# A convolution that feeds a mixture of experts: the third group's first stage moved ahead of the second sort, and what goes with it

## The chip, the cores and the metric

The kernel runs on one core of a Trainium2 chip. The metric is the device time of one execution in microseconds; the time of a kernel is the median of its runs. PE is the matrix engine (PEld its weight loads), DVE the vector engine, ACT the scalar engine, POOL the GpSimd engine. SP computes nothing here; it issues most of the DMA transfers, in the order of its queue. Every engine executes its own queue in order and waits there on semaphores.

## The reference, cut

Eight sequences of 5696 tokens of 128 channels are convolved causally with one filter per channel (by FFT in the reference). All 45568 tokens then go through a layer of eight experts, of which each token takes one.

```python
L = 2 * S
y = np.fft.irfft(np.fft.rfft(x, n=L, axis=1) * np.fft.rfft(h, n=L, axis=0)[None], n=L, axis=1)[:, :S]
t = y.reshape(B * S, D)
logits = t @ w_gate
expert_idx = np.argmax(logits, axis=1)          # gate_w = softmax probability of that expert
for e in range(E):
    mask = expert_idx == e
    out[mask] = gate_w[mask, None] * (np.maximum(t[mask] @ w1[e], 0.0) @ w2[e])
```

## The kernel before

The sequences are worked on in three groups of 2, 3 and 3. A sequence is laid out as a grid (48 by 119, padded to 120), so that the long Fourier transform becomes a transform over 120 points, one over 48 points and their inverses, all as matmuls. For each group there are these stages, which hand over through DRAM:

- `phase_a` (by `steps_a`): x to U, the first stage. An item is a quarter-slab of one sequence (`load` L287 brings `xt`, 240 KB; `cut` L278 splits it on ACT and DVE; `transform` L300 does three matmuls `pa` of 512 columns; `store` L309 copies `ut` by ACT and DVE). An item has two steps. When all sequences of a group have a slab, `flush` (L296) sends `ut` to U on SP, 720 KB at a time (L298).
- `phase_b`: U to V, the 48-point stage. Work goes by blocks `qb` of frequencies; `load_m` (L447) brings the matrices `mt`, by SP for the first two blocks of the third group and by POOL's queue behind them (`PLAIN` = 2); `load` (L468) brings `uq`, `mi` and the filter's spectrum `hh`, in two copies on the two halves of the partitions (L480). `forward` gives `xp` (two matmuls), `product` three DVE operations (L551, L560, L556), `combine` (L563) adds two of them, on DVE for the first `ALONE[g]` = (0, 14, 10) items and on POOL behind them, `inverse` gives `vp`, `save` (L591) has ACT copy it to `vt`.
- `phase_c`, the sort: V to tokens. `divide`, `synth` (matmul `yp`), `settle`, `turn`, `score` and `route` find each token's expert, `rank` (L872) finds its place and `sort` (L664) scatters the tokens there by POOL's indirect DMA. Behind every scatter but the last ones POOL sets a buffer to zero to pace the scatters (L896); this lies in `hh`'s third buffer, or in the first group in one of `mi`.
- `tables`: 12 short pieces of DVE work that make, from the counts per expert, the list of which tile of 256 tokens belongs to which expert.
- `experts`: a tile's tokens come as `xr`, an expert's weights as `wb` (SP, L1134). A step is one slice of 256 of the 1024 hidden units: `layer1` (`mh`), two relus (L1171 on ACT, L1173 on DVE), `layer2` (`ma`). A tile takes four steps, and there are 728 steps in all.

The first group's `phase_a` and `phase_b` come first. The first sort is then interleaved with the second group's `phase_a`. From there on `experts` runs beside `rest` (L1307), which does the second group's `phase_b`, the second sort, the third group's `phase_b` and the third sort. The third group's `phase_a` is a `Guest` (L351) of the second sort: it gets two steps (sometimes one) beside each piece of it, 72 in all. The interleaving is written out at build time: `run` (L1331) gives each stream a virtual time, and the next instructions are those of the stream that is behind. `HEAD` says when the experts start beside a group, `GAP` is a pause before the second and third sorts, in which only the experts get on, `SHARES` are the streams' shares.

In PSUM `vp` and `xp` share four banks (tag `cx`); the experts' `mh` has two banks of its own. `fcs` and `gcs` are constants of the two 120-point stages, read only at the beginning.

Of the kernel before, what the change touches and what calls it, by code (L numbers as in the profile page):

```python
# [23 lines left out]
NB = 48  # L24
# [3 lines left out]
HP = 64  # L28
# [23 lines left out]
ALONE = (0, 14, 10)  # L52
HEAD = (0, 5500, 9000)
# [13 lines left out]
TABLED = 4  # L67
RATE = (0.372, 0.55, 0.28, 0.8, 1.05, 0.6)
# [3 lines left out]
def conv_moe(ctx: ExitStack, tc: tile.TileContext, I, out, B, S, D, E, F, split):  # L72
# [86 lines left out]
    state = {"rests": False, "space": False, "spare": None, "pe": 0.0, "sent": 0.0, "tail": 0}  # L159

# [13 lines left out]
    fcs = load_const("fcs", [MP, 2, QN])  # L174
# [16 lines left out]
    gcs = load_const("gcs", [QN, 2, MP])  # L191
# [7 lines left out]
    jrow = load_const("jrow", [1, total])  # L199
# [66 lines left out]
    def steps_a(gr, tag, bufs):  # L266
        g, nb = gr.g, gr.nb
        srcs = [(I["x"][gr.b0 + b], b) for b in range(nb)]
        tw = 4 * D
        items = []  # L270
        for ig in range(NB // 4):
            for src, b in srcs:
                items.append((ig, src, b))
# [4 lines left out]
        def cut(n):  # L278
            if not split or n >= len(items):
                return  # L280
# [6 lines left out]
        def load(n):  # L287
            if n >= len(items):
                return
            ig, src, b = items[n]  # L290
# [18 lines left out]
        def store(m):  # L309
            n, c = divmod(m, 2)  # L310
            ig, src, b = items[n]
            if b == 0:
                uts[c] = sb.tile([QN, 4, gr.cols], F32, tag=tag, name=f"ut{g}_{ig}_{c}", bufs=bufs)
# [11 lines left out]
        def begin(m):  # L325
            if m == 0:
                cut(0)
            if m % 2 == 0:
                load(m // 2 + fore)
                cut(m // 2 + 1)  # L330
            transform(m)

        return start, begin, store, flush, 2 * len(items)

    def phase_a(gr):
        start, begin, store, flush, M = steps_a(gr, "six", SIX - gr.g)
        half = AT if gr.g == 0 else 750 * RATE[3 * gr.g - 3]
        start()
        for m in range(M + 2):
# [4 lines left out]
            yield half  # L344
# [6 lines left out]
    class Guest:  # L351
        def __init__(self, gr):
            self.start, self.step, self.store, self.flush, self.M = steps_a(gr, "mt", MT)
# [87 lines left out]
    def phase_b(gr):  # L441
# [26 lines left out]
        def load(qb):  # L468
# [8 lines left out]
            if g != 0:  # L477
                hhs[qb] = hhbufs[qb % 3]
                for k in range(2):
# [5 lines left out]
        state, banks, late = {}, {}, []  # L485

# [81 lines left out]
        def inverse(n):  # L568
# [4 lines left out]
            vp = ps.tile([P, 512], F32, tag="cx", name=f"vp{g}_{q}_{c}", bufs=4)  # L573
# [54 lines left out]
        for n in range(N + lags[3] + 2):  # L628
            qb, at = divmod(n, per)
            for k0 in range(at * PK, (at + 1) * PK):  # L630
                if k0 == 1:
                    load_m(qb + (3 if g == 0 else 2))
                if k0 == min(3, per * PK - 1):
                    load(qb + 2)
                if k0 == 0:
# [79 lines left out]
    def phase_c(pt, guest=None):  # L715
# [156 lines left out]
        def rank(n):  # L872
# [576 lines left out]
```

## Time and profile before

| | us |
|---|---|
| median of 3 runs | 2156.97 |
| lowest, highest run | 2149.70, 2160.83 |
| profiled execution, its own time | 2157.51 |
| its span in the trace | 2155.7 |
| PE busy in the span | 2082.7 |
| DVE busy | 1542.5 |
| ACT busy | 1114.9 |
| POOL busy | 1350.0 |

The span runs from the first to the last instruction of the trace. Stages in it: the first group until 229, the first sort and the second group's first stage from 229 to 391, the second group's 48-point stage from 394 to 685, a pause to 702, the second sort to 961, the third group's 48-point stage from 935 to about 1340, the third sort to about 1630, and experts alone behind it. A busy engine in the profile is one with an instruction in flight, and matmuls are pipelined: a row's count of instructions has to be read beside its busy time. In a row of instructions, the part in brackets is the idle time of the engine just before, and what ended it.

### The profile page before, as it was taken

The page shows a single profiled execution, that of the slowest core. Times are in us where ns is not written, and L with a number is a line of the kernel's source. Part 1 is how long each engine was busy: PE and PEld are TensorE (multiplying, and loading weights), DVE is VectorE, ACT ScalarE, POOL GpSimd, SP SyncE. Part 2 cuts the span into 40 slices and gives each one's busy share as a digit, 9 for nine tenths or more (in the row PEclk, how much of TensorE's full clock was granted, in tenths as well). Part 3 has the DMA queues.
Part 4 walks back from the last instruction along what each step waited for, and adds up shares of the span by engine and source line. Part 5 has one row for each costly group of instructions (what it writes and reads, how often), then busy time and mean ns, then how long its engine had stood idle before and what let it go on. Part 6 is the DMA issues. An engine that isn't in the chain of part 4 may idle for free.

```text
span 2155.7 us, 47101 instructions
## 1 busy us (share of the span) xinstructions
PE 2082.7 (97%) x14452; PEld 1863.3 (86%) x14452; DVE 1542.5 (72%) x3373; ACT 1114.9 (52%) x2317; POOL 1350.0 (63%) x1569
## 2 busy tenths in 40 slices
PE   9999999799999999989999999999999999999998
PEld 7799777377777889878888888999999999999998
DVE  4698677799997777688888887666665555555554
ACT  5677555143334666534555555555544454444544
POOL 6566388545554388888998775288883444443333
PEclk9999999599999999999999999999999999999999
DMA  8899799999997898868878885656533244343331
GB/s 269 263 289 293 227 297 281 256 237 256 248 267 196 232 276 255 245 168 229 204 205 222 216 203 153 159 132 159 141 103 98 87 132 135 129 133 126 123 121 34
DMA packets 216993, 420.33 MB, mean 195 GB/s; under 512 B 32501, under 2 KB 136235, under 8 KB 216740
## 3 DMA queue, kind: packets, MB, share of 16 engines
q1 hardware_dynamic: 187263, 360.52, 59.7%
q0 software_dynamic: 27072, 55.35, 8.9%
q8 instruction: 117, 1.92, 0.4%
q10 hardware_dynamic: 2405, 1.43, 0.2%
q14 instruction: 136, 1.11, 0.2%
HBM read 582.45 MB, written 154.27 MB: 342 GB/s over the span
## 4 chain that ended last, share of the span: by engine, by line
PE 82%; DMA 9%; DVE 3%; POOL 2%; issue 2%; ACT 1%; SPq 1%; ACTq 0%; POOLq 0%; DVEq 0%
PE mh L167 23%; PE ma L167 22%; PE vp L167 9%; PE xp L167 9%; PE yp L167 5%; PE mx L189 4%; PE pa L167 3%; DMA xt<-x 3%; PE gb L167 2%; DMA wb<-WD 2%; DMA mt<-mq 2%; PE tp L189 1%; PE hp L167 1%; PE lb L189 1%; DMA U<-ut 1%
## 5 line engine op out<-in xcount | busy, mean ns | idle before, releaser
L1173 DVE SCALAR_TENSOR_TENSOR hs<-mh,hs 128x512 fp32r<-128x512 f32 x728 | 501.6, 689 | 387.5 <-ACT hs L1171 381.2
L167 PE MATMUL mh<-xtb,wb 128*128 128x256 f32 x4368 | 706.4, 297 | 23.0 <-DVE hs L1173 5.2
L1171 ACT ACTIVATE hs<-mh 128x512 fp32r<-128x512 f32 x728 | 435.4, 598 | 488.1 <-PE mh L167 475.4
L167 PEld LDWEIGHTS mh<-xtb,wb 128*128 128x128 f32 x4368 | 589.8, 191 | 92.6 <-issue 37.9
L167 PE MATMUL ma<-hs,wb 128*128 128x256 f32 x4368 | 658.3, 287 | 1.7 <-DMA wb<-WD 1.7
L167 PEld LDWEIGHTS ma<-hs,wb 128*128 128x128 f32 x4368 | 574.4, 191 | 2.9 <-DMA wb<-WD 2.7
L665 POOL DMA_INDIRECT SR<-rt,pi x384 | 406.0, 1057 | 196.2 <-issue 58.9
L683 POOL DMA_INDIRECT out<-xr x310 | 305.4, 985 | 354.2 <-ACT hs L1171 172.6
L566 POOL TENSOR_TENSOR zt<-zt,xs 128x384 f32<-128x384 f32 (+1 forms) x276 | 295.8, 1074 | 155.2 <-DVE xs L556 103.9
L603 ACT COPY vt<-vp 96x384 f32<-96x384 f32 x240 | 114.2, 476 | 260.8 <-PE vp L167 256.6
L560 DVE TENSOR_TENSOR xs<-xp,hh 64x384 f32<-64x384 f32 (+1 forms) x360 | 214.8, 597 | 7.8
L167 PE MATMUL vp<-zt,mi 128*96 128x384 f32 x480 | 200.5, 500 | 0.0
L551 DVE TENSOR_TENSOR zt<-xp,hh 128x384 f32<-128x384 f32 (+1 forms) x300 | 173.6, 579 | 28.7 <-PE xp L167 18.4
L167 PE MATMUL xp<-uq,mt 96*128 96x384 f32 (+1 forms) x496 | 177.7, 462 | 8.5 <-DMA uq<-U 5.1
L167 PE MATMUL pa<-xc,fcr 120*120 120x512 f32 x576 | 159.4, 411 | 1.9 <-POOL xc L284 1.0
L556 DVE SCALAR_TENSOR_TENSOR xs<-xp,hh 64x384 f32<-64x384 f32 x240 | 134.3, 560 | 4.2
L167 PE MATMUL yp<-vr,gcr 120*120 120x384 f32 x576 | 119.5, 343 | 7.1 <-ACT ut L317 7.1
L167 PEld LDWEIGHTS vp<-zt,mi 128*96 128x96 f32 x480 | 79.7, 167 | 49.8 <-issue 26.7
L167 PEld LDWEIGHTS pa<-xc,fcr 120*120 120x120 f32 x576 | 99.9, 186 | 25.2 <-DVE rk L884 2.6
L167 PEld LDWEIGHTS xp<-uq,mt 96*128 96x128 f32 x496 | 87.6, 200 | 33.5 <-issue 12.8
L317 DVE COPY ut<-pa 120x512 f32<-120x512 f32 x96 | 65.7, 684 | 68.6 <-PE pa L167 54.7
L749 DVE TENSOR_TENSOR vr<-vq,vr 120x768 fp32r<-120x768 f32 x96 | 91.5, 954 | 31.8 <-ACT vr L748 31.0
(165 smaller groups left out, 2720.9 us busy)
## 6 DMA issues: line engine op xcount, KB each, us to landing
wb<-WD SPq DMA_DIRECT2D x728, 512.0 KB
U<-ut SPq DMA_DIRECT2D x48, 720.0 KB
uq<-U SPq DMA_DIRECT2D x60, 576.0 KB
V<-vt SPq DMA_DIRECT2D x60, 576.0 KB
vq<-V SPq DMA_DIRECT2D x48, 720.0 KB
xt<-x SPq DMA_DIRECT2D x96, 240.0 KB
hh<-HS SPq DMA_DIRECT2D x120, 192.0 KB
xr<-SR SPq DMA_DIRECT2D x155, 130.0 KB
```

What stands on the lines that cost most here:

```text
L167: nc.tensor.matmul(to, lhs, rhs, **kw)
L189: nc.tensor.transpose(dst, src, ident[:n, :n])
L551: nc.vector.tensor_tensor(out=zt, in0=x3, in1=hv[:, 0].broadcast_to([P, PK, cb, D]), op=ALU.mult)
L556: nc.vector.scalar_tensor_tensor(out=xs[to, 0], in0=x3[at, 0], scalar=-1.0, in1=him[:, 0], op0=ALU.mult, op1=ALU.mult)
L560: nc.vector.tensor_tensor(out=xs[to], in0=x3[at], in1=him, op=ALU.mult)
L566: eng.tensor_tensor(out=zt, in0=zt, in1=xs, op=ALU.add)
L603: done = nc.scalar.copy(outs_[qb][:, k0 : k0 + PK, c * cw : (c + 1) * cw], banks.pop(n)[:K2, :iw].rearrange("p (q x) -> p q x", q=PK),)
L665: s = nc.gpsimd.indirect_dma_start(out=SR[:, :], out_offset=IndirectOffsetOnAxis(ap=pi[:, b : b + 1], axis=0), in_=rt[:, b, :], in_offset= ...
L683: sc = nc.gpsimd.indirect_dma_start(out=out[:, :], out_offset=IndirectOffsetOnAxis(ap=xr[:, s, D + 1 : D + 2].bitcast(I32), axis=0), in_=x ...
L749: nc.vector.tensor_tensor(out=vr[:, 1], in0=src, in1=vr[:, 0].bitcast(F32), op=ALU.subtract)
L1171: done = nc.scalar.activation(hs[:, 0], hp, AF.Relu)
L1173: done = nc.vector.scalar_tensor_tensor(out=hs[:, 1], in0=hp, scalar=0.0, in1=hs[:, 0].bitcast(F32), op0=ALU.max, op1=ALU.subtract)
```

## The change

- The third group's first three items of `phase_a` (one slab, `AFORE` = 1) move from the guest to the end of the second group's `phase_a`, in the first sort, at double spacing (`SLOW`). The guest has 66 steps left.
- Of these the guest does eight in the pause ahead of the second sort, and it is through earlier in the sort. Once it is through, `phase_b` of the third group is begun (`ask`): its matrices and the inputs of its first two blocks are asked for, near the end of the sort.
- `ALONE` goes to (0, 5, 10), `HEAD` to (0, 7000, 9000): nine of the second group's combines go from DVE to POOL, and the experts begin two items later.
- From the third block on `hh` is loaded once, and its second half is made by ACT (`double`).
- The second group's `vp` takes the banks of `mh` as long as no expert has begun.
- The pacing memset writes the constants `fcs` and `gcs`, which lie in one tile `spent`, with 120 in place of 128 partitions and as many columns.
- `tables` is written anew: experts lie on nine partitions, sums over them are small matmuls with a new constant `tcol`; 14 pieces in place of 12.

```diff
-ALONE = (0, 14, 10)
-HEAD = (0, 5500, 9000)
+ALONE = (0, 5, 10)
+HEAD = (0, 7000, 9000)
+AFORE = 1
+SLOW = 2.0
...
-    fcs = load_const("fcs", [MP, 2, QN])
+    spent = const.tile([MP, 4, QN], F32, name="spent")
+    fcs, gcs = spent[:, :2], spent[:, 2:]
...
+        items = work(gr)[AFORE * nb :] if after else work(gr)
+        if g == 1:
+            items += work(groups[2])[: AFORE * groups[2].nb]
+        own = len(work(gr))
...
-            cp = nc.scalar.copy if c == 0 else nc.vector.tensor_copy
+            cp = nc.scalar.copy if c == 0 or n >= own else nc.vector.tensor_copy
...
-                late.append((gr.U[:, lo : lo + 4, :], uts[c]))
+                late.append((to.U[:, lo : lo + 4, :], uts[c]))
...
-            yield half
+            yield half * (SLOW if m >= own else 1)
...
-                for k in range(2):
+                for k in range(2 if qb < 2 else 1):
                     nc.sync.dma_start(hhs[qb][k * HP : k * HP + NB, :QB], HS[:, q : q + QB])
...
+        def double(qb, at):
+            if g and 2 <= qb < QN // QB:
+                hh = hhs[qb][:, at : at + QB // 2]
+                nc.scalar.copy(hh[HP : HP + NB], hh[:NB])
...
-            vp = ps.tile([P, 512], F32, tag="cx", name=f"vp{g}_{q}_{c}", bufs=4)
+            tag, bufs = ("mh", 2) if g == 1 and not live else ("cx", 4)
+            vp = ps.tile([P, 512], F32, tag=tag, name=f"vp{g}_{q}_{c}", bufs=bufs)
...
+        if ask:
+            yield 0
...
-                    idle = hhbufs[2].rearrange("p a b d -> p (a b d)") if g else mibufs[3].rearrange("p a x -> p (a x)")
-                    nc.gpsimd.memset(idle[:, : REST[g]], 0.0)
+                    nc.gpsimd.memset(spent.rearrange("p c q -> p (c q)")[:, : REST[g]], 0.0)
...
         load(0)
-        if gr.g:
+        for _ in range(4 if guest else 0):
+            guest.begin(2)
+            yield GAP / 4
+            guest.end()
+        if gr.g and not guest:
             yield GAP
         load(1)
...
+                if guest and (n, k) == (nu - 1, 1):
+                    assert guest.m == guest.M
+                    guest.bins = phase_b(guest.gr, True)
+                    next(guest.bins)
...
+        bank = ps.tile([P, 512], F32, tag="cx", name=f"ah{g}", bufs=4)
+        mm(bank[:E1, 0:1], tcol[:, 7 + E1 * down : 7 + E1 + E1 * down], nt, start=True, stop=True)
...
+        bank = ps.tile([P, 512], F32, tag="cx", name=f"rj{g}", bufs=4)
+        mm(bank[:1, :NT], tcol[:, 5:6], begun, start=True, stop=False)
+        mm(bank[:1, :NT], tcol[:, 6:7], ended, start=False, stop=True)
+        mm(bank[:1, 128 : 128 + NT], tcol[:, 5:6], over, start=True, stop=True)
+        mm(bank[:1, 256:257], nt, tcol[:, 1:2], start=True, stop=True)
```

## Rows read from the trace of the kernel before

**Rows 1.** The page, busy time by engine.
```profile
PE 2082.7 (97%) x14452; PEld 1863.3 (86%) x14452; DVE 1542.5 (72%) x3373; ACT 1114.9 (52%) x2317; POOL 1350.0 (63%) x1569
```

**Rows 2.** Windows: length; busy us (xcount) PE, PEld, DVE, ACT, POOL; clock; DMA; GB/s.
```profile
394.00:425.00 31.00, 26.49 (x38) 10.08 (x38) 27.03 (x67) 3.15 (x8) 14.08 (x18) 0.50 0.98 269
440.00:680.00 240.00, 239.62 (x1310) 177.89 (x1309) 226.33 (x416) 97.00 (x207) 137.81 (x137) 1.00 0.93 244
684.00:702.00 18.00, 14.62 (x102) 13.64 (x101) 7.64 (x13) 7.83 (x16) 0.97 (x1) 0.91 0.75 209
900.00:968.00 68.00, 55.80 (x343) 48.63 (x343) 51.77 (x156) 25.28 (x55) 58.51 (x82) 0.90 0.62 171
968.00:985.00 17.00, 13.36 (x75) 11.86 (x74) 13.18 (x26) 5.74 (x12) 11.70 (x12) 0.80 1.10 300
1700.00:1750.00 50.00, 50.00 (x427) 50.00 (x426) 27.93 (x50) 24.79 (x49) 23.69 (x25) 1.00 0.41 131
```

**Rows 3.** Groups by line, DVE, 440 to 680.
```profile
L556 DVE SCALAR_TENSOR_TENSOR xs<-xp,hh 64x384 f32<-64x384 f32 x104 | 58.2, 560 | 1.8
L1173 DVE SCALAR_TENSOR_TENSOR hs<-mh,hs 128x512 fp32r<-128x512 f32 x69 | 47.8, 692 | 2.2
```

**Rows 4.** Groups by line, POOL, 440 to 680.
```profile
L566 POOL TENSOR_TENSOR zt<-zt,xs 128x384 f32<-128x384 f32 x104 | 105.1, 1011 | 82.4 <-DVE xs L556 75.0 <-PE vp L167 4.2 <-PE ma L167 1.3
```

**Rows 5.** Timeline, end of the first sort: start, length, engine, line, operation, idle before.
```profile
385.26 1.23 SPq L473 DMA_DIRECT2D uq<-U  x1
391.02 0.23 PE L167 MATMUL gb_None<-oh,ones 120*128 120x54 bf16 x1 [1.41 <-DVE sm L866]
394.07 3.54 PE L167 MATMUL xp<-uq,mt 96*128 96x384 f32 x5 [2.72 <-DMA uq<-U]
396.15 0.56 DVE L551 TENSOR_TENSOR zt<-xp,hh 128x384 f32<-128x384 f32 x1 [2.35 <-DMA hh<-HS]
```

**Rows 6.** The chain that ended last.
```profile
920.36 7.98 DMA U<-ut
```

**Rows 7.** Timeline of DVE, the first and last of the tables' operations.
```profile
392.60 0.14 DVE L963 TENSOR_TENSOR cnt<-base,c_base 1x8 f32<-1x8 f32 x1
412.88 0.15 DVE L1056 TENSOR_TENSOR did<-did,nt 1x8 f32<-1x8 f32 x1
```

**Rows 8.** Timeline of PE, the second group's head.
```profile
414.31 1.65 PE L167 MATMUL xp<-uq,mt 96*128 96x384 f32 x2 [0.56 <-ACT vt L603]
417.80 1.65 PE L167 MATMUL xp<-uq,mt 96*128 96x384 f32 x2 [0.56 <-ACT vt L603]
```

**Rows 9.** Groups by line, the whole span.
```profile
L503 ACT ACTIVATE hh<-hp 64x512 f32<-64x512 f32 x120 | 70.9, 591 | 31.5 <-issue 16.6 <-ACT hh L503 8.6 <-PE hp L167 4.1
```

**Rows 10.** Timeline around the pause.
```profile
690.72 1.05 SPq L730 DMA_DIRECT2D vq<-V  x1
699.60 1.56 ACT L748 CAST vr<-vq 120x768 fp32r<-120x768 f32 x2
700.67 0.55 SPq L292 DMA_DIRECT2D xt<-x  x1
```

**Rows 11.** Groups by line, POOL, 700 to 965.
```profile
L665 POOL DMA_INDIRECT SR<-rt,pi x144 | 154.9, 1076 | 67.5 <-ACT hs L1171 40.6 <-issue 22.7 <-ACT xc L283 1.1
L896 POOL MEMSET hh<- 128x288 f32 x138 | 49.8, 361 | 0.2
```

**Rows 12.** Timeline at the second sort's end.
```profile
962.87 0.60 POOL L456 DMA_DIRECT2D mt<-mqs  x1
966.37 0.97 POOL L683 DMA_INDIRECT out<-xr  x1 [0.30 <-DMA mt<-mqs]
968.60 0.70 PE L167 MATMUL xp<-us,mt 96*128 96x384 f32 x3
```

**Rows 13.** SP's waits in total (us, times, longest); a row of PE's timeline.
```profile
SPq L480 <- POOL hh L896: 11.3, 1, 11.3
978.04 1.62 PE L167 MATMUL mh<-xtb,wb 128*128 128x256 f32 x6 [3.64 <-DVE xs L556]
```

More of the change, by code (lines that the diff above doesn't have):

```diff
@@ L264, in weights, with steps_a, work @@
             nc.sync.dma_start(*late.pop(0))
-    def steps_a(gr, tag, bufs):
+    def steps_a(gr, tag, bufs, after=False):
         g, nb = gr.g, gr.nb
-        srcs = [(I["x"][gr.b0 + b], b) for b in range(nb)]
         tw = 4 * D
[L270 to L273, printed above, removed]
+        def work(to):
+            return [(ig, I["x"][to.b0 + b], b, to) for ig in range(NB // 4) for b in range(to.nb)]
+        items = work(gr)[AFORE * nb :] if after else work(gr)
+        if g == 1:
+            items += work(groups[2])[: AFORE * groups[2].nb]
+        own = len(work(gr))
         xts, uts, xss = {}, {}, {}
@@ L278, in cut @@
         def cut(n):
-            if not split or n >= len(items):
+            if not split or n >= len(items) or n in xss:
                 return
@@ L330, in begin @@
                 cut(m // 2 + 1)
+                if m == 2 * own:
+                    cut(own + 1)
+                    cut(own + 2)
             transform(m)
-        return start, begin, store, flush, 2 * len(items)
+        return start, begin, store, flush, 2 * len(items), 2 * own
     def phase_a(gr):
-        start, begin, store, flush, M = steps_a(gr, "six", SIX - gr.g)
+        start, begin, store, flush, M, own = steps_a(gr, "six", SIX - gr.g)
         half = AT if gr.g == 0 else 750 * RATE[3 * gr.g - 3]
@@ L352, in __init__ @@
         def __init__(self, gr):
-            self.start, self.step, self.store, self.flush, self.M = steps_a(gr, "mt", MT)
+            self.start, self.step, self.store, self.flush, self.M, _ = steps_a(gr, "mt", MT, True)
             self.gr, self.m, self.open = gr, 0, []
@@ L961, in tables, with col @@
         down = pt.s % 2 == 1
-        cnt = sb.tile([1, E], F32, tag="cnt", name=f"cnt{g}")
-        nc.vector.tensor_tensor(out=cnt, in0=base[0:1, :E], in1=base0[0:1, :E], op=ALU.subtract)
-        ci = sb.tile([1, E], I32, tag="ci", name=f"ci{g}")
+        def col(name, n=1, dt=F32):
+            return sb.tile([E1, n], dt, tag=f"c_{name}", name=f"{name}{g}", bufs=1)
+        prior, at = state.get("done"), state.get("at", tcol[:, 3:4])
+        diag = col("diag", E1)
+        nc.vector.tensor_tensor(out=diag, in0=base[:E1], in1=ident[:E1, :E1], op=ALU.mult)
@@ L977, in tables @@
-        nc.vector.memset(end[:, none : none + 1], 0.0)
-        for k in range(E):
-            if k % 4 == 0:
-                yield
-            e = E - 1 - k if down else k
-            a, b = (e + 1, e) if down else (e, e + 1)
-            nc.vector.tensor_tensor(out=end[:, b : b + 1], in0=end[:, a : a + 1], in1=nt[:, e : e + 1], op=ALU.add)
-        yield
-        low, high = slice(0, E), slice(1, E + 1)
-        ahead, upto = (end[:, high], end[:, low]) if down else (end[:, low], end[:, high])
@@ L987, in tables @@
-        start = sb.tile([1, E + 1], F32, tag="start", name=f"start{g}")
-        nc.vector.memset(start, float(E * CAP))
-        here, after = (start[:, high], start[:, low]) if down else (start[:, low], start[:, high])
-        if prior is not None:
-            nc.vector.tensor_tensor(out=here, in0=prior, in1=ahead, op=ALU.subtract)
-        else:
-            nc.vector.tensor_scalar(out=here, in0=ahead, scalar1=-1.0, scalar2=None, op0=ALU.mult)
-        nc.vector.scalar_tensor_tensor(
-            out=here, in0=here, scalar=float(T), in1=base0[0:1, :E], op0=ALU.mult, op1=ALU.add
-        )
@@ L1049, in tables @@
             nc.vector.tensor_copy(state["left"], ej[:, NT - 1 :])
-        if not last:
-            did = sb.tile([1, E], F32, tag="did", name=f"did{g}")
+            did = sb.tile([E1, 1], F32, tag="did", name=f"did{g}")
             nc.vector.tensor_scalar(
@@ L1059, in tables @@
             state["done"] = did
+            state["at"] = const.tile([E1, 1], F32, name=f"at{g}")
+            nc.vector.scalar_tensor_tensor(
+                out=state["at"], in0=did, scalar=float(T), in1=tcol[:, 3:4], op0=ALU.mult, op1=ALU.add
+            )
     def begin(pt):
```

96 lines of the change are left out of this document (58 added, 38 removed).

## The prediction

> **What bounds the kernel now.** I read the page first: PE is busy for 97% of the span [rows 1]. That share alone says little, so next come windows, one for each stage. While the experts run alone, 50 us of "busy" PE hold 427 matmuls (8.5 per us); in the middle of the second group's convolution 240 us hold 1310 (5.5 per us), and PE is just as "busy" [rows 2]. There the grouping of DVE's work by line shows 104 items, each of three products of 0.55 to 0.56 us (the row of one is shown, the other two are alike) and 69 relus of 0.69 us [rows 3]: 3 x 58 + 48 + 14 of expert tiles' copies = 235 of 240 us. So DVE bounds that stage, although the window's own sum is 226. Its combine runs on POOL at 1.01 us each, where POOL has time [rows 4].
>
> The same windows show where PE loses: 8 us to the idle and to the half clock at the first sort's end and after it (394 to 425 at 0.50), 3.4 of 18 us in the pause before the second sort (684 to 702), 12.2 of 68 us at the second sort's end (900 to 968, at 0.90), and 3.6 of 17 behind it (968 to 985, at 0.80) [rows 2]. In the last two windows idle time and slow clock make 12.2 + 3.6 + 0.10 x 56 + 0.20 x 13 = 24 us. The change goes for these places, so I follow each in the timeline.
>
> The Trainium skill ("Trainium Kernel Development and Optimization", Performance Expectations) calls matmul busy time a bad metric, because matmuls are pipelined; the 1310 against the 427 matmuls bear it out [rows 2]. By the busy time, PE would bound the second group's convolution, term B below would be 0, and the sum would be 6 us higher.
>
> **A. End of the first sort: +8 us.** The second group's first stage now carries three more items of the third group, six steps of PE, at double spacing. They are queued on PE behind the sort's last matmul at 391.02 [rows 5], so their last copy leaves at about 393.6, and with it two stores of U of 720 KB. On SP's queue these stand ahead of the loads with which the convolution begins; uq went out at 385.26 before, and the first forward matmul began on its arrival at 394.07, the first product on hh's at 396.15 [rows 5]. Issued at some 394.5, behind 1.44 MB of stores and beside 0.8 MB of its own head, uq is there after 2.2 MB at the window's 269 GB/s [rows 2], 8 us, at 402 for 394: +8. Lower bound 0, if the six steps slip between the sort's last waits. Upper +16, if the load also has to wait until a store has landed, which took 7.98 us on the chain [rows 6].
>
> **B. The second group's convolution: -6 us.** ALONE falls from 14 to 5: nine combines go from DVE to POOL, 9 x 0.56 = -5.0 (a combine on DVE took what the product L556 takes [rows 3]). The tables: from cnt at 392.60 to did at 412.88 they took 7.4 us of DVE [rows 7]. The new ones are some 25 small operations at the last row's 0.15 = 3.7, so -3.7, and four tiny matmuls. Experts begin two items later (HEAD): 1.3 steps less in the stage, each with a relu of 0.69 [rows 3], -0.9. Together -9.6, if DVE bounds throughout. But in the head PE runs at the half clock: two forward matmuls took 1.65 us and an item's period was 3.49 [rows 8], against 2.3 of DVE's work per item, so of the savings that fall in the head about 3.6 meet PE instead: -6. Bounds -9.6 and 0. vp's move to the two banks of mh takes it out of xp's way; it is worth the 0.56 before such an xp, until experts are live, and lies inside these bounds. The second half of hh is copied by ACT now (56 per group; 0.59 each by the filter stage's ACT operation of as many columns that writes hh [rows 9]). ACT has 143 of 240 us free [rows 2], and DMA has 10.7 MB less to carry in the two groups: nothing, as long as the load is there early.
>
> **C. The pause: +4 us.** Eight steps of the third group's first stage stand ahead of the second load of vq. Each is three matmuls of 512 columns, 0.66 us, 5.3 in all; PE had 3.4 us idle in the 18 [rows 2]. So +2 if their inputs are there. These are asked for only behind vq's first load at 690.72 (the first xt went out at 700.67) [rows 10]. At the 8.9 us from vq's issue to its first use at 699.60 [rows 10], the last come at about 700, while ACT, which does their casts and copies in order, holds the relus behind them: another +2. Bounds 0 and +8.
>
> **D. The second sort: -2 us.** The guest's steps leave it (9.2 us of PE). But POOL was hardly waiting for PE there: its 144 scatters and 138 memsets took 154.9 + 49.8 us [rows 11] of the 231 from the first to the last, and the 26 us left are 0.18 for each scatter, the same from one to the next. It kept a pace of 1.60. After the last scatter POOL issues mt of the third block at 962.87, and the matmul that reads it starts at 968.60, 2.2 us after the landing at 966.4 [rows 12]. Whatever PE does sooner, that matmul, the ninth step of the third group, waits for POOL. So 2.2 us can go; 11 at most, if each scatter took 1.00 for 1.08 (an indirect DMA there took 0.97 [rows 12]); and 0 at least.
>
> **E. Third group's head: -2 us.** The first two blocks' loads are now issued before the sort is over, and SP no longer stands behind the memset on hh: before, hh's third load was held there for 11.3 us, weights came late behind it, and PE waited 3.64 us at 978.04 [rows 13]. That 3.64 can go; a restart from deeper idle at half clock takes 1.6 of it back (0.10 x 17). The early steps themselves only move idle time to before the ninth. Bounds -6.6 and 0. Here, too, the tables get shorter, but they run while POOL is waited for: 0.
>
> **F. Displaced expert steps: +2 us.** 1.3 steps that no longer lie beneath the second group's convolution are done at the end, at 50/427 x 13 = 1.52 us each [rows 2].
>
> The memset on `spent` has as many columns as before: 0. The consts load with the others at the start: 0. Sum: +8 - 6 + 4 - 2 - 2 + 2 = +4 us on the profiled execution's 2157.5, that is 2161.5. That execution is 0.5 us above the median, so 2161. What is late next is the ninth step of the third group, behind POOL.
>
> **Rivals.** *Faster, the third group's head is regained* (0.27). For it: 24 us lie open between 900 and 985, the memset's block on SP is real, and the U stores would be early if the six extra steps were done in the idle of PE between 386 and 394. Then 0 - 9.6 + 1 - 11 - 6.6 + 2 = -24, about 2133. Against: POOL's pace. It decides by whether mt of the third block still lands last.
> *Slower, U's stores stand before uq* (0.14). uq waits until the stores have landed, as it did in the third group's head (U<-ut 7.98 in the chain), A = +16; with the pause at +8, 16 - 6 + 8 - 2 - 2 + 2 = +16: 2173. From +5 in the stores' delay beyond my 8 it decides. For it: the chain of before passes through just such a store [rows 6]. Against: DMA could finish it beside the tables.
> *Slower, ACT's copies* (0.07). A copy that waits for its hh load holds the relus and vt behind it in a stage without slack on DVE; 28 blocks x 0.5 = +14 on +4: 2175.
> *It doesn't do what it says.* The sooner asking brings nothing, as the ninth step waits for the scatters: this is D of the forecast itself.
>
> **How the numbers follow.** Forecast 2161 with a chance of 0.52, its own range 2150 to 2172 by the bounds of A to C. The range reaches down to 2138, into most of the faster rival, and up to 2174. About 0.5% (10.8 us) is what a measurement of this kernel can tell: below 2146.2 is faster, above 2167.8 slower. Faster: 0.27 of the rival and a little of the forecast's lower edge, less the rival's upper edge, 0.27. Slower: 0.14 + 0.07 and 0.04 of the forecast, 0.25. Same: 0.48.
>
> **What would show it.** A: the first product of the second group at about 404, not 396, with U<-ut and uq in the chain. B: the stage from first product to last inverse 6 us shorter, DVE still 9.4 tenths or more. C: the first yp at 706 less what A and B made. D: scatters 1.53 to 1.60 apart, the matmul on mt of the third block within 2 us of its landing. E: no hh issue held on SP, no 3.6 us before mh behind the ninth step. I am wrong if uq leaves before 390, or if the 144 scatters run clearly faster than 1.53 apart.

## The result: 1.3% slower, and the profile after

The changed kernel takes 2184.32 us (median; 2181.78 to 2188.58) where the kernel before takes 2156.97: a ratio of 1.0134, 95% interval 1.0114 to 1.0153. Two more measurements of the same pair on other chips gave 1.0111 (1.0083 to 1.0138) and 1.0116 (1.0072 to 1.0159). The kernel before itself took 2157 to 2192 us on the chips of this study, so from here on a time is compared by its ratio to the kernel before on the same chip (in brackets the 95% interval), and stages by traces, best of one chip. The changed kernel did not run on the chip of x1 to x4; where their stages stand beside its own, the traces are of two chips. The changed kernel's span is 2181.9 us, 26.2 more than before.

I cut both spans at the same nine places, each read from the timeline of an engine (the first or last instruction of a kind), and set the forecast's terms beside the differences:

| from ... to | before | after | difference | forecast |
|---|---|---|---|---|
| start ... second group's first product (DVE) | 396.1 | 408.9 | +12.7 | A +8 |
| ... its last inverse `vp` (PE) | 289.1 | 281.5 | -7.6 | B -6 |
| ... first scatter of the second sort (POOL) | 45.2 | 67.0 | +21.8 | C +4 |
| ... its last scatter | 230.1 | 227.1 | -3.0 | D -2 |
| ... ninth step of the third group (`xp<-us`, PE) | 8.0 | 5.7 | -2.3 | D, E |
| ... its last product | 361.6 | 359.6 | -1.9 | E -2 |
| ... last scatter of the third sort | 288.4 | 287.0 | -1.4 | 0 |
| ... end | 537.0 | 545.0 | +7.9 | F +2 |

The last inverse is marked by the start of its row in the timeline, which holds one item before and two after; by the last item itself the two differences beside it are -7.0 and +21.2.

The page's busy times and the windows of the stages that answer to [rows 1, 2] (columns as there):

```profile
PE 2079.9 (95%) x14482; PEld 1866.2 (86%) x14482; DVE 1525.1 (70%) x3333; ACT 1185.9 (54%) x2432; POOL 1356.5 (62%) x1578
...
394.00:406.00 12.00, 0.00 (x0) 0.00 (x0) 0.00 (x0) 0.00 (x0) 10.21 (x15) 0.50 0.98 259
452.00:684.00 232.00, 232.00 (x1266) 172.71 (x1265) 217.71 (x400) 122.63 (x250) 133.49 (x133) 1.00 0.87 226
700.00:717.00 17.00, 12.64 (x66) 10.68 (x66) 6.70 (x12) 6.42 (x13) 0.00 (x0) 0.80 0.70 202
717.00:746.00 29.00, 19.13 (x111) 17.10 (x110) 11.91 (x20) 12.34 (x25) 0.00 (x0) 0.82 0.81 233
980.00:1007.00 27.00, 18.85 (x100) 15.99 (x99) 16.31 (x31) 9.27 (x19) 22.38 (x24) 0.71 0.70 176
1718.00:2168.00 450.00, 450.00 (x3806) 450.00 (x3805) 250.55 (x439) 221.21 (x439) 182.65 (x189) 1.00 0.36 114
```

PE is busy 2.8 us less than before in a span that is 26 us longer: over the whole span PE has no more to do, it waits. It does nothing between 394 and 406, and between 700 and 746 it is idle for 14.2 of 46 us at 0.80 to 0.82 of the clock, where before the whole pause lost 3.4 us of 18 [rows 2].

The first gap, in the timelines of SP, PE and DVE, answers to [rows 5]:

```profile
391.71 2.09 SPq L307 DMA_DIRECT2D U<-ut  x2
393.89 1.60 SPq L471 DMA_DIRECT2D mt<-mq  x1
395.59 1.63 SPq L485 DMA_DIRECT2D uq<-U  x1
391.35 0.21 PE L170 MATMUL gb_None<-oh,lt 120*120 120x54 bf16 x1
406.26 4.18 PE L170 MATMUL xp<-uq,mt 96*128 96x384 f32 x6 [13.43 <-DMA uq<-U]
408.88 0.56 DVE L568 TENSOR_TENSOR zt<-xp,hh 128x384 f32<-128x384 f32 x1 [14.96 <-DMA hh<-HS]
```

The sort's last matmul comes as early as before (391.07 there). But SP issues `uq` behind the two new stores, 10.3 us later than before, and it takes 10.7 us to arrive. The second gap, in the pause and behind it (SP, then PE, with ACT's wait between them), answers to [rows 10]:

```profile
698.13 1.06 SPq L754 DMA_DIRECT2D vq<-V  x1
703.09 0.88 SPq L301 DMA_DIRECT2D xt<-x  x2
706.50 3.22 PE L170 MATMUL pa<-xc,fcr 120*120 120x512 f32 x6 [4.15 <-ACT xc L292]
715.30 0.79 SPq L1165 DMA_DIRECT2D wb<-WD  x2
717.61 0.84 SPq L307 DMA_DIRECT2D U<-ut  x2
718.50 1.77 SPq L754 DMA_DIRECT2D vq<-V  x1
729.77 0.83 ACT L772 CAST vr<-vq 120x768 fp32r<-120x768 f32 x1 [9.16 <-DMA vq<-V]
731.03 0.86 PE L194 MATMUL tp<-ident,rt 120*128 120x120 f32 x3 [9.31 <-ACT rt L826]
```

The second load of `vq` went out at 699.71 before. Now it stands on SP behind an expert's weights (`wb`, 715.30) and behind two of the steps' stores of U, and it is used 11.3 us after its issue; PE stands 9.31 us. SP's waits in total (695 to 745: us, times, longest) show which of the two holds the queue:

```profile
SPq L1165 <- PE mh L170: 14.8, 2, 7.4
SPq L307 <- ACT vr L772: 0.3, 1, 0.3
```

The stores hardly wait for the copies that they send. The weights wait for PE's layer 1, whose matmuls of 709.51 and 714.39 came behind the step of 706.50, which had stood 4.15 us for its input. So the two waits of PE hang together. The second sort's scatters (POOL, grouped by line, 717 to 985) and the third group's ninth step answer to [rows 11, 12]:

```profile
L689 POOL DMA_INDIRECT SR<-rt,pi x144 | 152.3, 1058 | 91.2 <-ACT xc L292 64.8 <-issue 22.0 <-ACT hs L1203 0.9
L919 POOL MEMSET spent<- 120x288 f32 x138 | 49.9, 361 | 0.2
...
984.54 1.00 POOL L689 DMA_INDIRECT SR<-rt,pi  x1 [0.31 <-DMA SR<-rt,pi]
986.83 0.60 POOL L468 DMA_DIRECT2D mt<-mqs  x1
990.22 1.33 PE L170 MATMUL xp<-us,mt 96*128 96x384 f32 x3 [7.69 <-DMA mt<-mqs]
```

The scatters keep nearly the pace of before and PE now waits openly for what stands behind them on POOL.

### The profile page after: what moved, and what is told of

Read it like the earlier page. It is cut to its first block, busy times and chain, and to the rows that moved or that the text cites. A ratio compares the mean times of both kernels' runs of the same rounds, so it can differ in the third digit from the quotient of the medians.

```text
span 2181.9 us, 47199 instructions
## 1 busy us (share of the span) xinstructions
PE 2079.9 (95%) x14482; PEld 1866.2 (86%) x14482; DVE 1525.1 (70%) x3333; ACT 1185.9 (54%) x2432; POOL 1356.5 (62%) x1578
## 3 DMA queue, kind: packets, MB, share of 16 engines
q10 hardware_dynamic: 2439, 1.44, 0.2%
## 4 chain that ended last, share of the span: by engine, by line
PE 79%; DMA 8%; POOL 4%; DVE 3%; issue 2%; ACT 2%; SPq 1%; POOLq 0%; ACTq 0%; DVEq 0%
PE mh L170 22%; PE ma L170 22%; PE vp L170 8%; PE xp L170 8%; PE yp L170 4%; PE pa L170 4%; PE mx L194 3%; PE gb L170 2%; POOL SR L689 2%; DMA mt<-mq 2%; DMA xt<-x 2%; PE tp L194 1%; DMA SR<-rt,pi 1%; PE lb L194 1%; PE hp L170 1%
## 5 line engine op out<-in xcount | busy, mean ns | idle before, releaser
L583 POOL TENSOR_TENSOR zt<-zt,xs 128x384 f32<-128x384 f32 (+1 forms) x285 | 304.9, 1072 | 154.4 <-DVE xs L573 105.2
L170 PE MATMUL xp<-uq,mt 96*128 96x384 f32 (+1 forms) x496 | 172.8, 451 | 16.6 <-DMA uq<-U 13.4
L919 POOL MEMSET spent<- 120x288 f32 (+1 forms) x366 | 127.5, 348 | 0.5
```

The lines of the kernel that those rows point to most:

```text
L170: nc.tensor.matmul(to, lhs, rhs, **kw)
L583: eng.tensor_tensor(out=zt, in0=zt, in1=xs, op=ALU.add)
L919: nc.gpsimd.memset(spent.rearrange("p c q -> p (c q)")[:, : REST[g]], 0.0)
```

## The experiments

Each is the changed kernel with one edit, unless another base is named. Times are medians, with the ratio to the kernel before on the same chip.

### A: the stores ahead of `uq`

x2, the six steps at the sort's own spacing:

```diff
-SLOW = 2.0
+SLOW = 1.0
```

> The changed kernel with SLOW 1.0 for 2.0: the six extra steps of the first sort are spaced as the others and so come earlier in it, before its last pieces. Theory (uq behind the stores): the stores leave before the sort's last matmul, uq goes out near 386 to 388 and the first product of the second group comes at 397 to 400 in place of 408.88; the time falls by 9 to 12 us, to 2172 to 2175. Rival (the six steps' work and traffic): the sort's end moves back by as much as uq comes sooner, or the 1.44 MB of stores hold uq in any order; the time falls by 4 us at most.

Measured: 2207.74 us, ratio 1.0083 (1.0053 to 1.0112). From the sort's last matmul to the first product it took 11.8 us, against 17.5 in the changed kernel and 5.1 before; but the sort's last matmul came 143.2 us behind its first scatter instead of 134.8. In x1, x3 and x4, on the chip of x2 and with the spacing of the change, it came 134.8 to 140.8 behind, so between 2.4 and 8.4 us of this can be the steps'. The stall is moved at least in part, and the interval of the ratio overlaps with those of the changed kernel.

x8, no step of the third group in the first sort:

```diff
-AFORE = 1
+AFORE = 0
```

> The changed kernel with AFORE 0: no step of the third group in the first sort, all 72 with the guest, eight of them in the pause. Theory (A is the six steps and their stores): the first product of the second group is back at 396 to 398, 12 us sooner; the second sort takes the six steps beside its scatters for nothing; the time falls by 11 to 13 us. Rival (other parts of the change hold the head, as the new tables or hh's order): the first product stays above 403 and the time falls by 6 us at most.

x6, the changed kernel, on the same chip:

> The changed kernel itself, as it was, so that its trace and time stand beside the next three on one chip, since the kernel before took 2192 us on the chip of the last four runs. Every theory expects the first product of the second group some 12 to 13 us later than in the kernel before and a time 1.1 to 1.5% above it.

Measured: 2181.35 us, ratio 1.0054 (1.0027 to 1.0081), beside 2190.64 us, 1.0111 for the changed kernel (x6) on this chip: 9.3 us less by the medians. Last matmul to first product: 7.0 us, for 17.0 in x6. The first product itself came at 408.0, not at 396 to 398, as in this run the first sort had begun 8 us later; the place was misjudged by the start, the interval and the time bear the theory out. But the six steps were not free elsewhere: from the second group's last inverse to the first scatter this trace took 71.2 us for 66.3 in x6, and the scatters 230.8 for 226.5.

x5, the two stores issued by ACT:

```diff
             while late:
-                nc.sync.dma_start(*late.pop(0))
+                to, ut, own_ = late.pop(0)
+                (nc.sync if own_ else nc.scalar).dma_start(to, ut)
...
-                late.append((to.U[:, lo : lo + 4, :], uts[c]))
+                late.append((to.U[:, lo : lo + 4, :], uts[c], n < own))
```

> The changed kernel, but the two stores of U for the third group at the first sort's end are issued by ACT, which makes their copies, in place of SP. Theory (the order on SP): in the changed kernel SP issued uq at 395.59 behind those stores, for 385.26 before; now uq goes out near 386 to 388, the first product comes 9 to 12 us sooner than in the changed kernel, and the time falls by 9 to 12 us. Rival (the transfers themselves): 1.44 MB of stores at 259 GB/s hold the DMA engines for 5.6 us in any order, or ACT waits with the sort's operations behind its DMAs: the first product comes 0 to 4 us sooner.

Measured: 2186.80 us, ratio 1.0081 (1.0050 to 1.0111). Last matmul to first product: 7.0 us. So it is the order on SP that held the first `uq`, not the 1.44 MB. But the last inverse came at 689.4, as late as in x6 (688.8). SP's and PE's timelines show what stood in its place:

```profile
392.16 0.32 SPq L486 DMA_DIRECT2D uq<-U  x1
403.88 0.32 SPq L472 DMA_DIRECT2D mt<-mq  x1
406.28 0.32 SPq L486 DMA_DIRECT2D uq<-U  x1
...
399.86 4.18 PE L170 MATMUL xp<-uq,mt 96*128 96x384 f32 x6 [3.42 <-DMA uq<-U]
412.78 1.62 PE L170 MATMUL xp<-uq,mt 96*128 96x384 f32 x2 [7.04 <-DMA uq<-U]
```

The second block's `mt` and `uq` wait on SP until 403.88 and 406.28. Between 385 and 440 SP waits 5.1 us in all for U<-ut, in two waits. So the second block took the stall over, and the stores now end part of its wait. Why is not shown: what ended the wait until 403.88 the profile does not name, and in the kernel these loads' buffers have other tags (`mt`, `ld`) than the stores' source (`six`).

### C: the pause

x1, `vq`'s second load ahead of the steps:

```diff
         load(0)
+        if guest:
+            load(1)
         for _ in range(4 if guest else 0):
...
-        load(1)
+        if not guest:
+            load(1)
```

> The changed kernel, but the second load of vq is issued right behind the first, ahead of the eight steps of the pause. Theory (queue): in the changed kernel that load stood on SP behind two stores of U that waited for the pause's last copy, and went out at 718.50 instead of 699.71; PE then stood 9.31 us. The stall goes and the first scatter of the second sort comes at about 745 in place of 757; the time falls by 9 to 13 us, to 2171 to 2175. Rival (the steps themselves): the pause is late because eight steps and their inputs were put into it; the load only moves the waiting to xt and ACT; the time falls by 3 us at most, 2181 or more.

Measured: 2212.55 us, ratio 1.0105 (1.0072 to 1.0138); 67.3 us from the last inverse to the first scatter, for 67.0. My theory fell. The 9.31 us are gone, but the transfers that stand in front of the steps' inputs now cost the steps, and the weights still hold SP for up to 9.0 us until PE's layer 1 (PE's waits, 690 to 765: engine, what for, us in total, times, longest):

```profile
PE pa L170 <- ACT xc L292: 8.2, 1, 8.2
PE yp L170 <- ACT ut L326: 3.4, 1, 3.4
```

x3, the pause of before:

```diff
-        for _ in range(4 if guest else 0):
-            guest.begin(2)
-            yield GAP / 4
-            guest.end()
-        if gr.g and not guest:
+        if gr.g:
             yield GAP
```

> The changed kernel with the pause of before: no steps of the third group in it, all 66 of the guest lie in the second sort. Theory (the pause's steps cost, the sort hides them): from the second group's last inverse matmul to the first scatter it took 67.0 us in the changed kernel and 45.2 before; it is back at 45 to 50, the 144 scatters still take 227 to 231 us, and the time falls by 16 to 21 us, to 2163 to 2168. Rival (PE's work counts in the sort as well): eight steps of 0.66 us more lengthen the sort by 5 us; the time falls by 10 to 15 us.

Measured: 2199.52 us, ratio 1.0041 (1.0017 to 1.0064), the largest gain of any single edit. The interval is 56.9 us, and the scatters took 229.6 with all 66 steps beside them. Ten of C's 21.8 us are the eight steps, and this is the one edit whose interval lies clear of all three of the changed kernel's. But 57 is not 45, and PE's timeline names the rest:

```profile
713.03 1.62 PE L170 MATMUL mh<-xtb,wb 128*128 128x256 f32 x6 [6.68 <-DMA wb<-WD]
727.97 0.64 PE L194 MATMUL tp<-ident,rt 120*128 120x120 f32 x3 [3.55 <-ACT rt L826]
```

x18 keeps four of the eight steps, with x19, the changed kernel, on the same chip:

```diff
-            guest.begin(2)
+            guest.begin(1)
             yield GAP / 4
```

> The changed kernel with four steps of the third group in the pause in place of eight, those whose two inputs were asked for ahead of it; no store of U falls into the pause. Theory (the pause's steps cost by their inputs and stores, not by PE's time: PE stood 4.15 us for the third input and 9.31 us for vq behind the stores of U): from the second group's last inverse to the first scatter it takes 55 to 59 us, as with the plain pause (56.9 in x3), and the time is 8 to 12 us below the changed kernel's on the same chip. Rival (each step costs): 61 to 63, half of the way, and 4 to 6 us.

> The changed kernel as it was, for a trace and a time on the chip of x18. Every theory expects 66 to 67 us from the second group's last inverse to the first scatter of the second sort, 17 from the first sort's last matmul to the first product, and 1.011 to 1.014 of before.

Measured: 2181.81 us, 1.0077 (1.0048 to 1.0106), and 2190.25 us, 1.0116. The interval is 58.8 us, for 66.7. Four steps with inputs that are there, and no store of U among them, cost 2 us over the plain pause; the other four cost 8. The windows from the last inverse's end to the first scatter, before, in x3, in x18 and in the changed kernel, show of what this is made (columns as in [rows 2]):

```profile
686.08:730.50 44.42, 40.50 (x275) 37.57 (x275) 27.63 (x62) 26.43 (x54) 0.98 (x2) 0.96 0.86 231
698.08:753.54 55.46, 44.58 (x289) 41.10 (x289) 28.62 (x63) 26.59 (x54) 0.97 (x1) 0.91 0.73 197
692.41:749.78 57.37, 47.72 (x301) 43.84 (x301) 30.96 (x67) 28.78 (x58) 0.98 (x2) 0.88 0.75 218
691.87:757.42 65.55, 51.32 (x314) 46.05 (x313) 33.21 (x71) 30.45 (x62) 0.97 (x2) 0.87 0.74 211
```

PE's busy time grows with the steps, 44.6, 47.7, 51.3 us with none, four and eight, and its idle time goes 10.9, 9.7, 14.2. So of the ten us of the eight steps 6.7 are PE busy for longer, at a lower granted clock, and 3.4 are idle. The first four steps were laid into little of the idle time that was there, 1.2 us; the other four added 4.6 to it (5.0 against x19 on the chip of x18). Whether their inputs, their stores or the weights behind them bring that idle time was not tried one by one.

### HEAD: the other ten microseconds of the pause

x4, HEAD as before:

```diff
-HEAD = (0, 7000, 9000)
+HEAD = (0, 5500, 9000)
```

> The changed kernel with HEAD 5500 for 7000: the experts begin two items sooner beside the second group. Theory (displaced steps): at the third sort's last scatter the changed kernel had 15 matmuls of layer 1 fewer behind it than before, 2.5 steps, 3.9 us; they come back and the time falls by 3 to 4 us, to 2180 to 2181. Rival (DVE is the bound there): the second group's stage gets longer by the relus, 1 to 2 us, and the time falls by 0 to 2 us.

Measured: 2212.19 us, ratio 1.0109 (1.0074 to 1.0144). Neither theory held. 2068 matmuls of layer 1 were left behind the third sort's last scatter, for 2070 in the changed kernel: the displaced steps did not come back. Two stages moved against each other: first product to last inverse 287.7 us for 281.5, last inverse to first scatter 58.6 for 67.0. x11 and x12 show it without the moves of the third group.

x11:

```diff
-AFORE = 1
+AFORE = 0
...
-        for _ in range(4 if guest else 0):
...
-                if guest and (n, k) == (nu - 1, 1):
-                    assert guest.m == guest.M
-                    guest.bins = phase_b(guest.gr, True)
-                    next(guest.bins)
...
-            bins = guest.bins if guest else phase_b(gr)
+            bins = phase_b(gr)
```

> The changed kernel without its three moves of the third group: no step in the first sort (AFORE 0), none in the pause (the plain pause of before), and the third group's loads asked for where they were before. What is left is the second group's stage (combines on POOL, vp in the banks of mh, new tables, experts two items later), hh's half by ACT and the memset on spent. Theory (A and C carry the loss): from the second group's first product to its last inverse it takes 281 us, from there to the first scatter 45 to 50, and the time is 0.998 to 1.001 of the kernel before (-7.6 for the stage, +4 to +8 behind it). Rival (the rest costs too): from the last inverse to the first scatter it stays above 55, and the time is 1.004 or more.

x12, the same with HEAD 5500:

> The same with HEAD 5500, as before, so that the experts' steps and weight loads stand in the pause as they stood in the kernel before. Theory (the pause of x3 was long, 57 us from last inverse to first scatter, because weights were issued behind vq's first load and PE waited 6.68 us for them): the waits for weights in the pause are below 3 us, the interval is 45 to 48, the time 0.995 to 0.999 of before. Rival (HEAD has nothing to do with it): as the kernel without it, within 2 us.

Measured: 2197.92 us, 1.0041 (1.0014 to 1.0068), and 2193.05 us, 1.0018 (0.9993 to 1.0044). The second group's stage took 280.8 and 286.4 us, the interval behind it 56.2 and 46.3. SP and PE in the pause of x11, then of x12:

```profile
688.95 1.05 SPq L754 DMA_DIRECT2D vq<-V  x1
690.38 1.09 SPq L1157 DMA_DIRECT2D wb<-WD  x2
697.12 1.62 PE L170 MATMUL mh<-xtb,wb 128*128 128x256 f32 x6 [6.50 <-DMA wb<-WD]
```

```profile
687.04 1.83 SPq L1157 DMA_DIRECT2D wb<-WD  x2
690.68 1.05 SPq L754 DMA_DIRECT2D vq<-V  x1
692.61 0.93 PE L170 MATMUL mh<-xtb,wb 128*128 128x256 f32 x6 [1.66 <-DMA wb<-WD]
```

`vq` waits on SP for V's last store. With HEAD 5500 an expert's next weights go out ahead of that wait, with HEAD 7000 behind it, and PE stands 6.5 us. From the last inverse to the first scatter SP waits 13.9 us for PE's layer 1 in x11, 7.2 in x12 and 5.6 before. HEAD gains 6 us in one stage and loses 10 in the next. In the whole the medians are 4.9 us apart, and the intervals overlap. x11's theory fell and its rival held; x12's theory held for the interval of the pause, but its time did not come below the kernel before's. With x3 and x4 the four combinations stand at 46.3 us (HEAD 5500, plain pause), 56.2 (7000, plain; 56.9 in x3), 58.6 (5500, eight steps) and 67.0 (7000, eight steps): the two causes nearly add up.

### D and E: the second sort's end

x9, `mt` of the third block asked for ahead of the last scatters (with a guard in `load_m`, so that it is not loaded twice):

```diff
-        for qb in range(3 if g == 0 else 2):
+        for qb in range(3 if g == 0 or ask else 2):
             load_m(qb)
```

> The changed kernel, but mt of the third group's third block is asked for on POOL's queue together with the first two blocks, ahead of the last scatters of the second sort, in place of behind them. Theory (the ninth step waits for POOL): in the changed kernel the ninth step began at 990.22, 3.4 us after that load's issue, behind the last scatter at 984.54, and PE stood 7.69 us; now it begins 8 to 12 us sooner and the time falls by 5 to 8 us, as experts' steps fill part of it. Rival (DVE or the weights hold the head): PE stands elsewhere in the same stretch and the time falls by 2 us at most.

Measured: 2190.47 us, ratio 1.0100 (1.0064 to 1.0135); x6 on the same chip 2190.64. The ninth step comes 9.1 us ahead of the last scatter, 14.8 sooner than in x6 by that mark, and all of it is given back: from there to the last product 371.3 us for 358.2, and the 144 scatters took 232.8 for 226.5. PE's timeline and SP's waits (960 to 1010):

```profile
983.09 0.69 PE L170 MATMUL xp<-us,mt 96*128 96x384 f32 x3
1008.34 1.62 PE L170 MATMUL mh<-xtb,wb 128*128 128x256 f32 x6 [15.59 <-DMA wb<-WD]
```

```profile
SPq L1139 <- DMA out<-xr: 17.8, 1, 17.8
```

The experts' output scatters stand on POOL behind the sort's scatters as well; SP waits for one before it loads the next tile, and the weights wait behind that load. `mt` was one of several things that POOL's scatters hold.

x13, HEAD 5500, AFORE 0, the plain pause, and two guest steps with every piece, so that the early asking stays:

```diff
-                    guest.begin(1 if k == nsub - 1 and n >= 1 else 2)
+                    guest.begin(2)
```

> HEAD 5500, AFORE 0 and the plain pause, but the guest does two steps with every piece of the second sort, so that its 72 steps are over in time, and the third group's loads are asked for early as in the changed kernel. Theory (the sort hides the guest's steps, the early asking is worth what the changed kernel showed from the last scatter on, 2.3 + 1.9 us): 2 to 4 us less than the kernel without the asking (x12), or 0.993 to 0.998 of before. Rival (the denser steps lengthen the sort's start): from the last inverse to the first scatter 3 us or more above x12, and no gain.

Measured: 2209.16 us, ratio 1.0091 (1.0063 to 1.0119). The 144 scatters took 259.3 us for 233 to 235 in the runs beside it, and POOL stood up to 6 us between pieces, mostly released by ACT's relus. So at this density the sort does not hide the guest's steps; that PE falls behind there is my reading. Behind the last scatter the early asking did show: 5.8 us to the ninth step, for 21.5 in x12. The scatters took more than that away.

### The tables, and the end

x14 and x15, the kernel before with the new `tables` alone (and its constants), x0, the kernel before itself, beside x15:

> The kernel before with the new tables alone. Theory: DVE has 3.7 us less in the second group's head, of which one to three reach that stage's end; from the third sort's last scatter to the end it takes 537 us as before; the time is 0.998 to 1.000 of before. Rival (the new tables are slow where the third sort ends): that last interval is 540 to 545, as in every run with the change, and the time is 1.000 to 1.003 of before.

> The kernel before itself, as it was, for a trace beside the next three on one chip. Every theory expects a ratio of 1.00 and the stages of the first trace: 230 us for the 144 scatters, 8 from the last of them to the ninth step, 537 from the third sort's last scatter to the end; if these come out at 234, 20 and 545 as in the last four runs, the chip made them, not the new tables.

> The kernel before with the new tables alone, once more, beside a trace of the kernel before. Theory (the new tables tie DVE to PE: sums over experts are matmuls, queued on PE behind experts' matmuls, and DVE stands in order until they are done): from the last scatter of the second sort to the ninth step 12 to 15 us more than before on the same chip, at the end 4 to 8 us more, the time 1.003 to 1.006 of before. Rival (the chip of those runs): both intervals as in the kernel before within 2 us, a ratio of 0.999 to 1.001.

Measured: x14 2198.45 us, 1.0052 (1.0025 to 1.0079); x0 2181.43 us, 0.9977 (0.9943 to 1.0012); x15 2196.89 us, 1.0051 (1.0022 to 1.0080). From the third sort's last scatter to the end x0 took 544.3 us and x15 545.7, from the second sort's last scatter to the ninth step 13.5 and 15.7. So the kernel before alone has 537 or 544, 8 or 13.5. The kernel before had 2052 and 2058 (x0) matmuls of layer 1 left behind that last scatter, the changed kernel 2070 in each of its three traces: 12 to 18 more, 2 to 3 steps of six, 3.0 to 4.6 us at 1.52 us a step [rows 2]. On the chip of x0 the changed kernel with the old tables (x16, below) has 544.5 us there for 544.3, on the first chip it is 545.0 for 537.0. How much of the "8 us of the end" the change costs is therefore open between nothing and 8. The new tables cost 0.5% in both runs; where is not settled: in the second group's stage they gain (first product to last inverse 287.4 us for 289.0, and 285.4 in x14 on another chip), and of the 15 us between the medians the two traces show 4. x15's theory had the time right and the place wrong: 2.2 us more up to the ninth step, for 12 to 15. x14's DVE shows one long wait in the second sort's new tables, at the operation that takes up the small matmuls `rj`:

```profile
977.53 0.21 DVE L1014 SCALAR_TENSOR_TENSOR r<-c_jrow,rj 1x67 f32<-1x67 f32 x1 [10.77 <-PE ma L167]
```

PE had those matmuls done at 970.9, so they were not what ended it; in the changed kernel the same operation followed them by 0.4 us without a wait. x15 and x11 wait there too, 6.0 and 10.1 us, and behind matmuls that were done; the three traces of the changed kernel do not. What held DVE stays open.

x16, the changed kernel, and x17, the kernel of x12, each with the old tables:

> The changed kernel with the tables of before. Theory (the end's 8 us are 3.9 of displaced experts' steps and 4 of the new tables): from the third sort's last scatter to the end 3 to 5 us less than with the new ones, 541 for 545; the second group's stage 1 to 3 us longer; the time 1 to 4 us less than the changed kernel, 1.011 to 1.013 of before. Rival (the tables gain 3.7 us in the second group and cost nothing behind it): 2 to 4 us more than the changed kernel.

> The kernel of x12 (combines on POOL, vp in the banks of mh, hh's half by ACT, memset on spent, HEAD 5500, no move of the third group) with the tables of before. Theory (what is good of the change is the second group's stage): five us of combines less, nothing lost behind it: 0.996 to 0.999 of before. Rival (hh's copies on ACT or the memset cost as much): 1.000 to 1.003.

Measured: 2209.32 us, 1.0103 (1.0058 to 1.0149), and 2183.96 us, 0.9994 (0.9972 to 1.0016). Neither is told from its pair with the new tables (1.0111 and 1.0116; 1.0018). What is left of the change in x17, the combines on POOL, `vp` in the banks of `mh`, `hh`'s half by ACT and the memset, is worth 3.6 us in the second group's stage (285.4 for 289.0, one trace each) and nothing that can be measured in the whole. No version was found that beats the kernel before.

## Why the prediction was wrong, point by point

**C failed, and it alone puts the time outside the range.** It was put at +4 with an upper end of +8 and measured +21.8; with C at +4 and all else as measured the time would be 2166.5. Two steps of its working were wrong. The first is the overlap: I set the eight steps' 5.3 us of PE against the 3.4 us in which PE was idle there. That idle time was not theirs to use. From the plain pause of x3 to the changed kernel PE's busy time between the last inverse and the first scatter rose from 44.6 to 51.3 us, and its idle time, 3.9 before, rose from 10.9 to 14.2. PE stood 4.15 us for a step's input and 9.31 for `vq`, which SP issued only behind the weights and the steps' stores. I had written that the steps stand ahead of `vq`'s second load and did not price it. Moving that load does not mend it (x1): the eight steps cost 10 us in either order (x3), four cost 2 (x18). The second is a term that I put at nothing. I took HEAD as a matter of the experts' number, -0.9 in B and +2 in F. It also moves the place in the experts' cycle at which the pause begins, and so put the weights behind `vq`'s wait: +10 (x11 against x12), of which 5.7 are idle time of PE and 4.2 busy, one step of the experts more among it.

**A: the mechanism was right, the size was off.** +12.7 for +8, inside its bounds. I had `uq` issued at 394.5, it was 395.6; I had 8 us to its arrival, it was 10.7. x8 and x5 show that the steps' stores held `uq`, and by the order on SP. What they cost later, in x5's second block, is not explained. (The 8 us that I read off 394 to 425 do not come out of the row, which has 4.5 us idle and the rest at half the clock; no term uses them.)

**B: -7.6 for -6, with the wrong shares: the size was partly luck.** DVE stays nearly full (100 items of three products, 67 relus and the tiles' copies: 3 x 56 + 46 + 13 of 232 us, as in [rows 3]). But combines, `vp` and `hh` gave 3.6 together (x17 against x0), the tables 1.6 (x15) or 3.7 (x14), and HEAD the most, 6, of which I had 0.9. With HEAD at 7000 the stage holds two steps of the experts fewer (438 matmuls of layer 1 for 450). Two relus on DVE are 1.4 us and two steps on PE 3.0, so neither engine's time explains 6, and that DVE alone bounds the stage is not shown. The shares do not add up to a sum: all but HEAD together (x12) made the stage 286.4 for 289.0. PE is "busy" for 232.00 of 232 us there, and x17, with as many of the experts' matmuls in the stage as x0, still made it shorter. The Trainium skill ("Trainium Kernel Development and Optimization", Performance Expectations) calls matmul busy time a bad metric, and this trace agrees. The prediction's counts of 5.5 and 8.5 matmuls per us overstate the gap, though: `xp` and `vp` have 384 columns and the experts' matmuls 256, and counted in columns the two windows hold some 1580 against 2100 per us.

**ACT's copies of `hh`: nothing, as forecast.** In 232 us of that stage 49 copies took 30.3 us and waited 1.8 us for `hh`'s load; ACT was busy for 123. That rival is out.

**D and E went the way that was forecast, and further.** The scatters and what stands behind them gained 3.0 + 2.3 us for the 2 forecast, the stage behind it 1.9 for 2. The point on which they rested, that the ninth step waits for `mt` behind POOL's scatters, shows in the row of 990.22; and x9 showed more than I had: with that wait gone, others on POOL hold the same stretch. From the last scatter to the ninth step every kernel that asks early, but x9, took 5.5 to 6.0 us on all chips; the others took 8.0 to 23.4. On the chip of x0 that step came 6.0 us behind the last scatter in x16 and 13.5 in x0. So the first pair, with 8.0 before, shows the early asking at its smallest. SP no longer stood at `hh`'s third load (11.3 us in [rows 13]). That weights held PE at 978.04, as E had it, is not what that row says: it names a product on DVE.

**F: +2 forecast, 3.0 to 4.6 by the matmuls left.** That HEAD displaces them, as I had it, is not shown: x4, with HEAD of before, leaves 2068. Of the +7.9 of the table, the rest is no more than the kernel before's own spread between 537 and 544.

**The rivals.** The faster one is out: POOL held the third group's head. The slower one with U's stores in front of `uq` (2173) was the nearest in kind, but its price was put on the landing of a store instead of on SP's order, and its pause was priced at 8. The one with ACT's copies (2175) was nearer in time, and its reason is the one that the trace rules out.

## What to carry to other kernels

Work that is moved into a pause costs its engine time, unless the trace shows that it can stand in the very gaps that are there, and it brings its loads and stores with it: write out the issuing queue of that stretch in order, with each wait, and price what comes last behind the last wait. A constant that shifts when a periodic stream starts also shifts where in its cycle every later pause falls; look at which of its loads then stands behind a blocking one. Where one queue (here POOL's 144 scatters) sets the pace of a stage, work taken from another engine there is worth little (3.0 us of 230 here), and removing one of the waits behind it only shows the next.

## What the runs showed that I had not expected

The same kernel takes 2157 to 2192 us on different chips, and not evenly: the second sort's end to the ninth step took 8.0 us in one trace of the kernel before and 13.5 in another, the stage up to the third sort's last scatter 288.4 and 296.9, the end 537.0 and 544.3, while experts alone ran at 3815 matmuls in 450 us in both. A term of a few microseconds that is read from one trace is not a property of the kernel until a second trace shows it.
